# Batch 0's first two tiles as a pair, and later or closer o tiles for batches 2, 3 and 4, in a fused attention and MLP kernel

## The chip, the cores and the metric

One core of one Trainium2 chip. The metric is the device time of one execution in microseconds (us). The kernel before takes 290.79 us (three runs, 290.41 to 290.98).

Engines: PE is TensorE, PEld its weight loads, ACT is ScalarE, DVE is VectorE, POOL is GpSimd, SP is SyncE (here it only issues DMAs).

## The reference

```python
# q, k, v: (8 batches, 8 heads, 576, 64)
kv  = einsum('bhsd,bhse->bhde', k, v)
o   = einsum('bhsd,bhde->bhse', q, kv)
x   = o / sqrt(mean(o*o, -1) + 1e-6) * g_norm        # then (8, 576, 512)
xn  = (x - mean(x)) / sqrt(var(x) + 1e-6) * g_ln
out = x + relu(xn @ w_ch1) @ w_ch2                    # 512 -> 2048 -> 512
```

## The kernel before

Each batch's 576 rows are four tiles of 128; the last 64 rows of two batches make a leftover tile. For each tile, PE computes o from the turned q (`qt`) and the batch's kv. DVE and ACT make x and the centred xc from it. xc is turned to `xT`, for early batches by PE, from batch 2 on by a DMA. `mm1` (line 413) multiplies xT by w1, `mm2` (line 429) the relu by w2. POOL issues the loads of later batches; before each set it copies one element of every tile that has to be ready first (`gate`, line 98), so the copy shows when that tile landed.

An agenda decides when a batch's side work is put among the matmuls of another. `tick()` is called once per slot, about 0.87 us of matmuls:

```python
def at(slot, fn):
    agenda.setdefault(int(slot), []).append((slot, fn))   # the fraction only orders inside a slot

def plan_tile(s, make, turn_at, on_pe):
    ...
    at(s, first)          # o on PE, square on ACT, sum on DVE
    at(s + 2, second)     # root on ACT; reciprocal, y, x, xc on DVE
    at(s + 6, third)      # variance square on ACT
    at(turn_at, fourth)   # xc -> xT

def turn_q_dma(b):
    q_p = kv_in.tile([128, JJ, H, D], bf16, tag="qp", bufs=2)
    nc.vector.tensor_copy(q_p.rearrange("p j h d -> p h j d"), q_in[b % NB])     # line 203
    q_t = qt_pool.tile([128, JJ, HP, 128], bf16, tag="qt", name="qt")
    nc.sync.dma_start_transpose(...)                                             # line 205
```

```python
def mm1(b, t0, n, c0=0, c1=nDe):          # n tiles together, column blocks c0 to c1 of w1
    ...
    per = 4 // n
    for de0 in range(c0, c1, per):
        tick()
        p1 = ps1.tile([128, per, n * 128], f32, tag="p1", name="p1")   # three buffers
        for i in range(per):
            for kk in range(nK):
                nc.tensor.matmul(p1[:, i, :], lhsT=w1_sb[...], rhs=blk[2][:, kk, sl], ...)
        nc.scalar.activation(m1[:, de0:de0 + per, sl], p1, func=AF.Relu)
```

## Time and profile before

| | before |
|---|---|
| time, median of 3 | 290.79 us |
| span of the profiled run | 288.8 us |
| PE busy | 280.9 us, 97% |
| DVE, ACT busy | 149.8 us, 153.2 us |
| waits of PE over 0.2 us after 19 us | four, 1.3 us together |

PE bounds the kernel. The other engines have half their time free, but each tile's chain runs through ACT, DVE and a DMA, and must be ready when PE comes to it. The prediction shows the lines.

A wait of PE is here the excess of the distance between two matmul starts over the usual distance for that shape, unless it is said to be by the profile's count; the profile counts from a matmul's recorded end, which is later, and so gives less.

### The profile page before, as it was taken

What the parts mean: (1) busy time and instruction counts of PE and PEld (TensorE: products, weight loads), DVE (VectorE), ACT (ScalarE), POOL (GpSimd) and SP (SyncE); (2) the same over time, 40 slices, a digit from 0 to 9 for tenths busy, and PEclk for the clock granted to TensorE, in tenths of its full rate; (3) what the DMA queues carried; (4) which work ended last, traced back from release to release, by engine and by line L of the source; (5) the groups of instructions that cost most, each with busy time, mean ns of one, the idle gap of its engine ahead of it and who ended that gap; (6) DMA issues with size and microseconds to landing.
All of it is one profiled execution on the core that took longest, in us unless ns stands there. A gap on an engine that the chain in (4) does not pass through costs nothing.

```text
span 288.8 us, 5753 instructions
## 1 busy us (share of the span) xinstructions
PE 280.9 (97%) x2295; PEld 157.9 (55%) x2295; DVE 149.8 (52%) x331; ACT 153.2 (53%) x333; POOL 41.0 (14%) x69
## 2 busy tenths in 40 slices
PE   7889999999999999999999999999999999999994
PEld 3579756995479644444444444444444444444444
DVE  5774119938897783764376935762578200220022
ACT  3477844985379733872288318921893066016400
POOL 8522510041005004100500032000000000000000
PEclk9999999999999999999999999999999999999999
DMA  7999999979788959996994189947203410230033
GB/s 214 199 206 205 198 190 195 214 112 193 138 173 101 194 108 157 202 159 120 157 217 68 39 152 219 155 84 149 56 18 64 101 36 0 48 81 19 0 73 75
DMA packets 67546, 36.76 MB, mean 127 GB/s; under 512 B 35516, under 2 KB 62524, under 8 KB 67520
## 3 DMA queue, kind: packets, MB, share of 16 engines
q0 software_dynamic: 28528, 17.76, 43.8%
q1 hardware_dynamic: 38480, 17.91, 31.2%
q10 hardware_dynamic: 512, 0.72, 0.7%
q8 instruction: 18, 0.29, 0.4%
q14 instruction: 8, 0.07, 0.1%
HBM read 36.71 MB, written 9.44 MB: 160 GB/s over the span
## 4 chain that ended last, share of the span: by engine, by line
PE 85%; DMA 5%; DVE 5%; ACT 2%; issue 1%; SPq 1%; DVEq 0%; POOLq 0%
PE p L413 41%; PE p L429 37%; PE o_ps L271 2%; DMA v_in<-in_v_dram 2%; DMA qt<-q_p 2%; PE kv_ps L246 2%; DMA xT_blk<-xc 1%; DVE ss L298 1%; ACT m L416 1%; DVE x_blk L322 1%; DVE y L303 1%; DVE o_sb L434 1%; PE p L198 1%; SPq L205 1%; ACT rms L308 0%
## 5 line engine op out<-in xcount | busy, mean ns | idle before, releaser
L413 PE MATMUL p<-xT_blk,w_sb 128*128 128x128 bf16 (+2 forms) x1024 | 131.6, 286 | 0.6 <-DMA xT_blk<-xc 0.2
L429 PE MATMUL p<-w_sb,m 128*128 128x512 bf16 (+2 forms) x608 | 129.1, 368 | 0.0
L416 ACT ACTIVATE m<-p 128x512 bf16<-128x512 f32 x144 | 85.2, 596 | 43.0 <-PE p L413 40.5
L413 PEld LDWEIGHTS <-w_sb 128*128 128x128 bf16 x1024 | 78.7, 98 | 44.9 <-issue 1.5
L429 PEld LDWEIGHTS <-m 128*128 128x128 bf16 x608 | 57.0, 98 | 62.0
L434 DVE SCALAR_TENSOR_TENSOR o_sb<-p,rstd,x_blk 128x512 f32<-128x512 f32 (+2 forms) x38 | 27.3, 720 | 52.2 <-PE p L429 41.2
L277 ACT ACTIVATE sq<-o_ps 128x512 f32<-128x512 f32 x35 | 20.9, 596 | 41.7 <-PE o_ps L271 41.7
L298 DVE TENSOR_REDUCE ss<-sq 128x8 f32<-128x512 f32 x35 | 23.7, 678 | 13.0 <-ACT sq L277 12.9
L340 ACT ACTIVATE dev<-x_blk,st_blk 128x512 f32<-128x512 f32 x36 | 25.7, 714 | 6.2 <-DVE st_blk L326 6.1
L332 DVE SCALAR_TENSOR_TENSOR xc<-x_blk,st_blk,g_ln_sb 128x512 bf16<-128x512 f32 x34 | 25.6, 752 | 1.2
L303 DVE TENSOR_TENSOR y<-o_ps,inv 128x512 f32<-128x512 f32 x33 | 22.8, 692 | 3.4 <-PE p L413 0.5
L322 DVE SCALAR_TENSOR_TENSOR x_blk<-y,g_norm_sb 128x512 f32<-128x512 f32 x33 | 22.8, 692 | 1.1
L315 DVE RECIPROCAL inv<-rms 128x8 f32<-128x8 f32 x36 | 7.2, 201 | 23.0 <-ACT rms L308 23.0
L422 DVE RECIPROCAL rstd<-rstd 128x4 f32<-128x4 f32 x9 | 1.6, 175 | 31.2 <-ACT rstd L421 31.1
L308 ACT ACTIVATE rms<-ss,eps_sb 128x8 f32<-128x8 f32 x36 | 10.7, 296 | 11.5 <-DVE ss L298 11.4
L98 POOL COPY gate<-qt 1x1 bf16<-1x1 bf16 x5 | 0.9, 177 | 106.4 <-DMA qt<-q_p 106.4
L271 PEld LDWEIGHTS <-qt 128*128 128x128 bf16 (+1 forms) x156 | 10.2, 100 | 8.1 <-issue 1.7
L271 PE MATMUL o_ps<-kv_pack,qt 128*128 128x128 bf16 (+1 forms) x156 | 13.7, 220 | 0.2
L198 PE MATMUL p<-fill_sb 128*128 128x512 bf16 x27 | 8.0, 448 | 1.2 <-DVE eps_sb L137 1.2
L340 ACT ACTIVATION_READ_ACCUMULATOR dev<-x_blk,st_blk 128x1 f32 x36 | 6.8, 189 | 0.0
L249 ACT CAST kv_pack<-kv_ps 64x256 bf16<-64x256 f32 x7 | 2.6, 366 | 7.7 <-PE kv_ps L246 7.7
L246 PEld LDWEIGHTS <-k_in 128*64 128x64 bf16 x280 | 5.0, 112 | 2.6 <-issue 2.5
(80 smaller groups left out, 110.5 us busy)
## 6 DMA issues: line engine op xcount, KB each, us to landing
out_dram<-o_sb SPq DMA_DIRECT2D x70, 128.0 KB, 2.4
w_sb<-in_moe_w_ch_dram POOLq DMA_DIRECT2D x8, 512.0 KB, 15.2
q_in<-in_q_dram POOLq DMA_DIRECT2D x7, 320.0 KB, 12.3
k_in<-in_k_dram POOLq DMA_DIRECT2D x7, 320.0 KB, 6.0
v_in<-in_v_dram POOLq DMA_DIRECT2D x7, 320.0 KB, 8.6
q_in<-in_q_dram POOLq DMA_DIRECT2D x8, 256.0 KB, 12.3
k_in<-in_k_dram POOLq DMA_DIRECT2D x7, 256.0 KB, 6.7
v_in<-in_v_dram POOLq DMA_DIRECT2D x7, 256.0 KB, 10.6
```

The lines of the kernel that those rows point to most:

```text
L198: nc.tensor.matmul(p1, lhsT=fill_sb[:, :128], rhs=fill_sb, start=True, stop=True)
L271: nc.tensor.matmul(flat[rows, hp * 128:(hp + 1) * 128], lhsT=lhsT_of(hp), rhs=kvp[:, hp, :], start=True, stop=True)
L277: nc.scalar.activation(self.sq_t, self.o_ps, func=AF.Square)
L298: nc.vector.tensor_reduce(self.ss, self.sq_t, axis=AX.X, op=ALU.add)
L303: nc.vector.tensor_mul(self.y_t, self.o_ps, self.inv().to_broadcast([128, H, D]))
L322: nc.vector.scalar_tensor_tensor(x_blk[:, ts].rearrange("p (h d) -> p h d", h=H), in0=self.y_t, scalar=1.0, in1=g_norm_sb.to_broadcast([12 ...
L332: nc.vector.scalar_tensor_tensor(self.xc_t, in0=x_blk[:, self.ts], scalar=st[:, 1, self.ts:self.ts + 1], in1=g_ln_sb, op0=ALU.add, op1=ALU ...
L340: nc.scalar.activation(dev, x_blk[:, ts], func=AF.Square, bias=st[:, 1, ts:ts + 1], accum_out=st[:, 2, ts:ts + 1])
L413: nc.tensor.matmul(p1[:, i, :], lhsT=w1_sb[:, kk, de * 128:(de + 1) * 128], rhs=blk[2][:, kk, sl], start=(kk == 0), stop=(kk == nK - 1))
L416: nc.scalar.activation(m1[:, de0:de0 + per, sl], p1, func=AF.Relu)
L429: nc.tensor.matmul(p2[:, c0:c1], lhsT=m1s[b][:, de, ts * 128:(ts + 1) * 128], rhs=w2_sb[:, de, c0:c1], start=(de == 0), stop=(de == nDe - 1))
L434: nc.vector.scalar_tensor_tensor(o_sb[:, c0:c1], in0=p2[:, c0:c1], scalar=rstds[b][:, ts:ts + 1], in1=blks[b][0][:, ts, c0:c1], op0=ALU.mu ...
```

## The change

Its intent, as I read it from the diff: fewer and wider matmuls in batch 0, and tiles of batches 2 to 4 placed so that the turned q is there when PE wants it, and batch 3's tiles are done before batch 4's q has to be copied.

```diff
-    for j, s, tn in ((0, 45, 51), (1, 49, 55), (2, 53, 61), (3, 57.5, 64)):
+    for j, s, tn in ((0, 45.7, 51.5), (1, 49.5, 55), (2, 53, 61), (3, 57.5, 64)):
         plan_tile(s, lambda j=j: main_tile(2, j), tn, False)
...
-            o = s + d + (11 if b == 3 else 13) + 5 * j
+            o = s + d + (11.7 + 4.4 * j if b == 3 else (14 if b == 4 else 13) + 5 * j)
...
-    for ts, c0, c1 in ((0, 0, 4), (1, 0, 4), (0, 4, 8), (1, 4, 8), (0, 8, 12), (1, 8, 12),
-                       (2, 0, 12), (0, 12, 16), (1, 12, 16), (2, 12, 16), (3, 0, 16)):
-        mm1(0, ts, 1, c0, c1)
+    for ts, n, c0, c1 in ((0, 1, 0, 4), (1, 1, 0, 4), (0, 2, 4, 12), (2, 1, 0, 12),
+                          (0, 2, 12, 16), (2, 1, 12, 16), (3, 1, 0, 16)):
+        mm1(0, ts, n, c0, c1)
```

## The prediction

> **What bounds the kernel now.** I read the views in this order: the page's totals and slices, the groups of instructions kept apart by shape, the chain of work that ended last in order of time, then the timeline of single engines in the stretches where that chain leaves TensorE.
>
> ```profile
> PE 280.9 (97%) x2295; PEld 157.9 (55%) x2295; DVE 149.8 (52%) x331; ACT 153.2 (53%) x333; POOL 41.0 (14%) x69
> PE   7889999999999999999999999999999999999994
> PEclk9999999999999999999999999999999999999999
> ...
> L413 PE MATMUL p<-xT_blk,w_sb 128*128 128x128 bf16 x512 | 31.2, 219 | 0.4
> L413 PE MATMUL p<-xT_blk,w_sb 128*128 128x256 bf16 x128 | 14.6, 273 | 0.0
> ...
> 19.53 2.69 PE p L413 x48
> 29.41 3.73 PE p L413 x64
> 83.50 4.37 PE p L413 x40
> ```
>
> TensorE (PE) is busy for 97% of the span at full granted clock; from the fourth slice on no slice is below 9 tenths before the last. The mean times 219 and 273 ns are not what a matmul costs: the matmuls overlap. The cost is the distance from one start to the next, and the chain gives it: 48 matmuls of 128 columns take 2.69 us, 56.0 ns each; 40 of 256 columns take 4.37 us, 109.2 ns each. (The 64 in 3.73 us contain one wait of 0.2 us; 3.57 us is the clean figure for 64 elsewhere in the same chain, 55.8 ns.) So only two things can shorten this kernel: less matmul time, or fewer gaps on PE. After the start-up (18 us) I compared every distance between matmul starts with that of its shape. The real waits are four: about 0.24 us at 25.1, 0.21 at 29.15, 0.21 at 82.8, and 0.66 in two pieces at 111.1 to 112.25. They sum to 1.3 us, 0.45% of the time. That is the ceiling for a change that only moves work.
>
> The largest of them:
>
> ```profile
> 106.53 3.10 SPq L205 DMA_TRANSPOSE qt<-q_p  x1
> 109.69 1.26 SPq L352 DMA_TRANSPOSE xT_blk<-xc  x1
> ...
> 111.63 0.40 PE L271 MATMUL o_ps<-kv_pack,qt 128*128 128x128 bf16 x4
> 112.25 1.02 PE L413 MATMUL p<-xT_blk,w_sb 128*128 128x512 bf16 x4 [0.23 <-DMA xT_blk<-xc]
> ...
> 109.69 2.52 DMA xT_blk<-xc
> ```
>
> PE ends batch 2's second product at 111.36, waits for the turned q of batch 4 (qt), does the first o tile of batch 4 (0.22 us) and waits again, for the turned last tile of batch 3 (xT), which lands at 112.21. The SP queue issues qt first and is held 3.1 us by it; so xT is late because qt is, and qt is late because its source, the copy q_p on VectorE (DVE), is:
>
> ```profile
> 98.41 1.50 DVE L298 TENSOR_REDUCE ss<-sq 128x8 f32<-128x512 f32 x2
> 99.83 0.19 DVE L315 RECIPROCAL inv<-rms 128x8 f32<-128x8 f32 x1
> ...
> 103.10 0.19 DVE L315 RECIPROCAL inv<-rms 128x8 f32<-128x8 f32 x1
> ...
> 105.65 0.82 DVE L203 COPY q_p<-q_in 128x2560 bf16<-128x2560 bf16 x1
> ```
>
> From 95.78 to 105.65 DVE has no gap: tiles 2 and 3 of batch 3 and the leftover tile, one after the other.
>
> **What the Trainium skill says.** "TensorE: Matmul & The Clock Gate", section "Wait — 56ns, not 53.3ns?": warm matmuls start N ÷ 2.4 GHz plus about 2.5 ns apart. For 128 columns that is 55.8 ns and for 256 it is 109.2; the trace agrees (55.8 to 56.0, 109.2). So a pair saves one fixed cost of 2.5 ns and nothing more. The same page, "Architectural detail", says that ScalarE (ACT) and DVE take their instructions in strict order; so the order in the program decides, and the trace shows it: ACT's root for tile 2 of batch 3 starts at 95.46, though its sum was ready at 94.32, because a relu and another root stood ahead. "Perfetto Trace Analysis", section "DMA Instruction — HWDGE (DVE, Sync)", says that the recorded time of such an issue doesn't contain the data's movement. The trace agrees: xT's issue took 1.26 us, its landing 2.52.
>
> **The change part by part.**
>
> Part one, the pair. Batch 0's tiles 0 and 1 do 12 of their 16 column blocks of w1 together: 12 x 4 = 48 matmuls of 256 columns in place of 96 of 128. The slots stay 16 and every slot uses the same chunk of w1 as before. Chunks 1, 2 and 3 land at about 17.2, 19.7 and 22.2 us (semaphore arrivals in the trace); their first use is at 19.4, 21.2 and about 26.3. No new wait. The gain is 2 x 55.9 - 109.25 = 2.55 ns per pair, 0.12 us in all. But the slot that starts at 22.5 is followed by the wait at 25.1: ACT did a copy, a square and a root there that waits for DVE's sum, and PE lacks a free product buffer until the next relu. That chain starts with the slot, so its 8 pairs (0.02 us) only lengthen the wait. 40 pairs count: -0.10 us. The waits at 25.1 and 29.15 stay, as what they wait for is untouched. The relus have the same 512 columns.
>
> Part two, batch 2. The agenda runs a function in the whole slot of its number; the fraction only orders functions inside the slot. 45 to 45.7 and 49 to 49.5 therefore move no o tile. Comparing the instruction order of the two kernels engine by engine confirms it: PE's order differs only by the pairs and from batch 3 on; on ACT the roots of tiles 1 and 2 come ahead of the squares for the variance. Those roots start at 68.82 and 73.15, within 0.04 us of the sums that they wait for; the squares had ended at 68.26 and 71.99. So nothing was blocked: 0.00 us. The wait at 82.8 (qt of batch 3, landing at 83.06) stays too, as its o tile stays in slot 66 (66.7).
>
> Part three, batches 3 and 4. Tiles 2 and 3 of batch 3 go from slots 76 and 81 to 75 and 79; the slot is 0.87 us. Tile 2's sum can't come sooner: DVE ends tile 1 at 93.72. But its root now stands behind one relu less and ahead of rstd: right after the variance square, at about 94.79 in place of 95.46. Then on DVE, with the distances measured before: reciprocal at 95.11; 2.63 us to the end of the tile, 97.74; rstd 0.18; tile 3's sum 0.68, ready at 98.62; now a bubble of 0.36 for its root, which used to run beneath the leftover tile's sum; reciprocal at 98.98; 2.61 us, 101.59; the leftover's sum 0.68; the output product 0.66; its reciprocal at 102.93, before 103.10. So q_p, qt and xT come only 0.17 us sooner: xT at 112.04. Meanwhile the first o tile of batch 4 moves from slot 96 to 97. Its 0.22 us lay inside the wait and was free; now it comes after, and costs. -0.17 + 0.22 = +0.05 us. Later stages show no wait: q of batch 5 is turned before 138.5 and used at 141.4.
>
> Sum: -0.10 + 0.00 + 0.05 = -0.05 us. 290.79 - 0.05 = 290.7.
>
> **The rivals.** First, the intent: the tiles closer together free q_p enough that the wait before batch 3's first product ends, and the o tile's later slot keeps qt off the path. For it: 0.66 us is waited there and xT would need to come only 0.7 us sooner than now. Against: DVE has no gap to give back, only the order changes. It would make 290.79 - 0.10 - 0.66 + 0.22 = 290.25. Second, ACT becomes the bound: at 4.4 slots a tile it has 4.4 relus of 0.54, a square 0.55, a variance square 0.8 and a root 0.3, about 4.0 us in 4.1. PE has three product buffers of slack and ACT is idle again from slot 80 on; if it fails, the wait moves into 90 to 96 and costs up to 0.5: 291.2. Third, the extra bubble on DVE is longer than 0.36, q_p is later than before, and the wait grows: 291.0.
>
> **Range and chances.** Three runs before lie within 290.41 to 290.98, so run to run is +-0.3. The rivals lie at -0.5 and +0.4. Range 290.1 to 291.2 for 8 in 10. Two per cent is 5.8 us, over four times all the waits after the start-up, and nothing added costs more than a few tenths: faster 0.01, same 0.98, slower 0.01.
>
> **What would show it.** The shape table: 416 matmuls of 128 columns and 176 of 256. The waits near 25.1 and 29.1 still there, everything from 29.5 on some 0.1 us sooner. o of batch 3's first tile still starts as qt lands. q_p of batch 4 0.2 to 0.3 us sooner than 105.65, and one wait near 111.3 to 112 before the first 512-column product, with xT as its releaser. If that wait is gone, or q_p is 0.5 us sooner or later than I say, step three is wrong; if PE gaps appear at 90 to 96, the second rival holds.

## The result, and the profile after

The changed kernel takes 292.53 us (four runs, 292.24 to 293.57) against 290.60 (four runs). The ratio is 1.0072, 95% interval 1.0044 to 1.010. Ratios here are the mean time of one kernel's fast runs over that of the other's fast runs of the same rounds, so not quite the ratio of the medians. It is slower by 1.9 us: within 2%, but clearly outside the predicted range, which ended at 291.2.

The page of the changed kernel, totals and the PE row of its slices, then its first products by shape (count, busy us, mean ns):

```profile
PE 279.2 (96%) x2222; PEld 157.2 (54%) x2247; DVE 149.6 (51%) x331; ACT 152.6 (52%) x333; POOL 41.4 (14%) x69
...
PE   8689999999989997999999999999999999999994
...
L413 PE MATMUL p<-xT_blk,w_sb 128*128 128x128 bf16 x416 | 25.7, 219 | 0.4
L413 PE MATMUL p<-xT_blk,w_sb 128*128 128x256 bf16 x176 | 20.5, 273 | 0.0
```

The counts 416 and 176 are as planned. Two slices in the row of nines have fallen: an 8 at 80 to 88 us and a 7 at 109 to 117. (Some single matmuls are missing from this trace: PE has 25 fewer than PEld. A distance of exactly two matmuls is such a hole, not a wait.)

The first of these places in the timeline of the kernel before:

```profile
78.09 3.21 SPq L205 DMA_TRANSPOSE qt<-q_p  x1
83.11 0.40 PE L271 MATMUL o_ps<-kv_pack,qt 128*128 128x128 bf16 x4
```

Both places in the changed kernel's timeline, and from the chain of waits the turned last tile of batch 3:

```profile
79.07 3.94 SPq L205 DMA_TRANSPOSE qt<-q_p  x1
84.83 0.40 PE L271 MATMUL o_ps<-kv_pack,qt 128*128 128x128 bf16 x4 [0.79 <-ACT m L416]
84.91 0.18 POOL L98 COPY gate<-qt 1x1 bf16<-1x1 bf16 x1 [17.58 <-DMA qt<-q_p]
...
111.02 1.26 SPq L352 DMA_TRANSPOSE xT_blk<-xc  x1
114.94 1.04 PE L413 MATMUL p<-xT_blk,w_sb 128*128 128x512 bf16 x3 [1.69 <-DMA xT_blk<-xc]
...
111.02 3.87 DMA xT_blk<-xc
```

PE waits 0.95 us for the first o tile of batch 3 in place of 0.21, and 1.85 us between batch 2's second product and batch 3's first; before, that gap was 0.89 us and held an o tile of 0.22. The profile names an ACT relu as the first wait's releaser. But POOL's gate, which waits for the turned q alone, passes at the same moment, 0.08 us later; q landed 5.7 us after its issue. This is the case of several conditions of which the last named is not the guilty one.

The compute chains are not late. Counted from the first o tile of batch 3, the copy q_p of batch 4 comes 22.17 us later (107.00 - 84.83), before 22.54 (105.65 - 83.11). It is the transfers that took longer: the turned q of batch 4 6.6 us in place of 5.1, the turned tile 3.87 in place of 2.52. The view of line 205 (six turned q; the profile gives the landing of five of them before and of four after) shows, before and then after:

```profile
DMA to landing us min/median/max: 4.9/5.0/5.1
```

```profile
DMA to landing us min/median/max: 5.0/5.5/6.6
```

The account from first product to last matmul: before 14.95 to 284.86, 269.91 us; after 16.13 to 287.79, 271.66 us. That is +1.75. Of it -0.09 is the pair stage (18.03 to 17.94 us), +0.74 the first wait, +0.96 the second gap (1.85 - 0.89), +0.22 the o tile that now comes after it: +1.83. The 1.2 us by which this one profile starts later is not in the other three runs, whose spans are 290.5 to 290.8 us.

What slowed the transfers? The page lists a DMA queue of kind "instruction": 18 transfers of 16 KB before (q8), 17 after. These bring PE its program, as the paddings below bear out. The Trainium skill, "Runtime: NRT & Kernel Launch", section "Instruction fetch mechanics", says that programs are refilled in blocks of 16 KiB, 256 instructions, over a DMA queue of the engine's own. The trace agrees in the main: PE's recorded matmuls and weight loads are 4590 before, and 4494 after with each load's matmul counted, 17.9 and 17.6 blocks; the sequencer's own instructions are not in these counts. Taking out 96 instructions moves every later refill. The records of that queue start before at 74.4, 89.2 and 102.8 us, all clear of the turned q of batches 3 (78.1 to 83.1) and 4 (106.5 to 111.6). After, they start at 78.9 and 112.4, beside both. (A second queue of this kind, q14, moves pieces of 8 KB; in none of the traces does one fall inside a turned q.)

The DMA view, 3 us each, begins as batch 3's q is turned: the kernel before from 78.0, the changed one from 78.8. Rows are 40 slices of the mean busy share of 16 engines, and of GB/s.

```profile
DMA  9896959559998969533799999999999999999999
GB/s 218 218 300 137 300 109 246 137 137 246 273 218 164 218 137 273 109 58 51 133 236 208 256 191 246 188 232 171 242 201 212 198 225 208 229 212 225 215 218 215
```

```profile
DMA  0966996969299979992400100000001599999999
GB/s 0 218 164 164 218 218 137 246 137 246 82 246 219 273 164 218 191 246 55 110 0 0 27 0 0 27 27 27 27 27 14 106 195 229 222 222 201 225 212 208
...
q8 instruction: 1, 0.02, 2.5%
```

Before, the dip in the middle is three slices long. After, eleven slices (0.8 us) hold almost nothing: at most a tenth of the engines move, and then all resume together. In the second place (111 to 115 us of the changed kernel) the rate is 8 to 10 GB/s for most of 1.2 us, where the whole set gives over 200: about what one engine in sixteen gives.

```profile
GB/s 220 210 218 220 200 225 218 205 220 205 185 111 54 148 376 212 195 207 177 72 8 0 0 0 8 10 8 10 10 10 8 21 0 0 123 123 82 225 123 246
...
q8 instruction: 1, 0.02, 1.5%
```

This reads as one DMA engine that had the 16 KB refill to do (1.0 to 1.2 us for each of these two) and finishes its share of the turning late, while the other fifteen are done and the transfer counts as landed only with the last. The packet times in the trace fit: the refill of the second place ends at 113.40 us, and from then to 114.17 the turning's packets of 256 bytes end one after the other, some 0.03 us apart. The Trainium skill, "DMA: Bandwidth & Descriptors", section "Issuing engines are not separate DMA queues", says that transfers from different issuers run on the same 16 engines and interleave. Up to here all this is reading. The experiments follow.

### The profile page after: what moved, and what is told of

It reads as the page before. It is cut to its first block, busy times and chain, and to the rows that moved or that the text cites. A ratio compares the mean times of both kernels' runs of the same rounds, so it can differ in the third digit from the quotient of the medians.

```text
span 291.8 us, 5633 instructions
## 1 busy us (share of the span) xinstructions
PE 279.2 (96%) x2222; PEld 157.2 (54%) x2247; DVE 149.6 (51%) x331; ACT 152.6 (52%) x333; POOL 41.4 (14%) x69
## 4 chain that ended last, share of the span: by engine, by line
PE 67%; DMA 17%; issue 10%; DVE 2%; POOL 1%; ACT 1%; SPq 0%; DVEq 0%; POOLq 0%
PE p L413 33%; PE p L429 32%; DMA v_in<-in_v_dram 8%; DMA w_sb<-in_moe_w_ch_dram 5%; DMA q_in<-in_q_dram 3%; PE o_ps L271 2%; DMA xT_blk<-xc 1%; PE kv_ps L246 1%; DVE o_sb L434 1%; DVE ss L298 0%; SPq L205 0%; ACT m L416 0%; DVE q_p L203 0%; DVE x_blk L322 0%; DVE y L303 0%
## 5 line engine op out<-in xcount | busy, mean ns | idle before, releaser
L429 PE MATMUL p<-w_sb,m 128*128 128x512 bf16 (+2 forms) x592 | 126.7, 368 | 1.4 <-issue 0.8
L413 PEld LDWEIGHTS <-w_sb 128*128 128x128 bf16 x976 | 77.7, 98 | 47.2 <-DMA xT_blk<-xc 2.2
L298 DVE TENSOR_REDUCE ss<-sq 128x8 f32<-128x512 f32 x35 | 23.7, 678 | 15.4 <-ACT sq L277 15.4
L246 PE MATMUL kv_ps<-v_in,k_in 128*64 128x64 bf16 x280 | 5.8, 197 | 0.0
```

The lines of the kernel that those rows point to most:

```text
L246: nc.tensor.matmul(kv_ps[hh * D:hh * D + D, hp, :], lhsT=k_in[b % NB][:, h, j, :], rhs=v_in[b % NB][:, h, j, :], start=(j == 0), stop=(j = ...
L298: nc.vector.tensor_reduce(self.ss, self.sq_t, axis=AX.X, op=ALU.add)
L413: nc.tensor.matmul(p1[:, i, :], lhsT=w1_sb[:, kk, de * 128:(de + 1) * 128], rhs=blk[2][:, kk, sl], start=(kk == 0), stop=(kk == nK - 1))
L429: nc.tensor.matmul(p2[:, c0:c1], lhsT=m1s[b][:, de, ts * 128:(ts + 1) * 128], rhs=w2_sb[:, de, c0:c1], start=(de == 0), stop=(de == nDe - 1))
```

## The experiments

Theory R: the loss comes from the refills, moved by the 96 removed PE instructions onto transfers that PE waits for. Rival S: the moved slots cost it. Each run below was timed beside the kernel before on the same chip, and gave correct results.

**The pair alone.** All slots as before, batch 0 as after.

```diff
-        mm1(0, ts, 1, c0, c1)       # before's list of single tiles
+        mm1(0, ts, n, c0, c1)       # the changed kernel's list
```

> Part one alone: batch 0's pair, all agenda slots as before. PE has 96 instructions fewer than before, as the changed kernel has. Theory R (PE's instruction refills, 16 KB each, one per 256 PE instructions, come at other moments and slow the turning transfers they meet): nearly all of the loss is here, 291.6 to 292.4 us, with a refill near 78 to 79 and another near 110 to 113, the wait before batch 3's first o tile 0.7 to 1.0 us in place of 0.21, and the wait before batch 3's first product over 1 us. Rival S (the moved slots cost it: tiles closer together, the o tile no longer hidden): 290.5 us, no longer wait anywhere.

Measured: 291.93 us (six runs) against 290.60, ratio 1.0049 (1.0034 to 1.0064). Refills at 78.6, 97.6 and 114.9; batch 3's q lands 5.9 us after issue and PE waits 1.16 us for it. Batch 4's q lands in 5.0 and the wait at 111 to 114 is short; that part of the expectation missed, and so did the refill expected near 110 to 113. Instead PE waits elsewhere (the profile's timeline of PE):

```profile
102.28 0.82 PE L246 MATMUL kv_ps<-v_in,k_in 128*64 128x64 bf16 x40 [0.38 <-DMA v_in<-in_v_dram]
...
173.49 0.40 PE L271 MATMUL o_ps<-kv_pack,qt 128*128 128x128 bf16 x4 [0.45 <-DMA qt<-q_p]
```

The first is the load of v for batch 4. Its second part was issued 1.1 us later than in the kernel before (this profile's first product is 0.8 us late, and POOL's gates on batch 3's turned q and batch 2's turned tile passed later), and it took 9.5 us in place of 8.1, with the refill of 97.6 inside it. The second is batch 6's q, issued at 166.8, with a refill at 171.4, landing in 6.6 us. The part that saves matmul time loses 1.3 us, most of the changed kernel's 1.9; the two intervals overlap, so the rest is not told apart.

**The slots alone.** Batch 0 as before, agenda as after.

```diff
-        mm1(0, ts, n, c0, c1)       # the changed kernel's list
+        mm1(0, ts, 1, c0, c1)       # before's list
```

> Parts two and three alone: the moved slots, batch 0 without the pair. PE has as many instructions as before. Theory R: 290.4 to 290.9 us, refills at the same moments as before within 0.5 us, turned q of batches 3 and 4 landing 5.0 us after issue. Rival S: 292 to 292.6 us, with the refills where they were and the waits of the changed kernel.

Measured: 290.39 us (five runs), ratio 0.9994 (0.9982 to 1.0007). All turned q with a recorded landing (five of six) land in 4.9 to 5.1 us. Rival S falls.

**The changed kernel with 96 PE instructions put back.** They are tiny matmuls on zeros while PE idles for its first loads.

```diff
-    fill(18)
+    fill(14)
+    small(52)     # 52 matmuls of 64 columns into an unused PSUM tile: 104 PE instructions, less the 8 of 4 fills
```

> The changed kernel with 96 PE instructions put back as tiny matmuls of 64 columns on zeros while PE idles for the first loads (4 of the 18 warming matmuls give way), so that refills meet the same work as before. Theory R: 290.3 to 290.8 us, refills near 74.4, 89 and 102.8, the two long waits gone back to 0.2 and under 0.7 us. Rival S: 292.5 us as the changed kernel.

Measured: 290.54 us, ratio 0.9999 (0.9987 to 1.001). Refills at 74.4, 89.1 and 103.0; the turned q land in 4.9 to 5.1 us; the waits are 0.21 us, and 0.56 us for the turned tile (0.39 by the profile's count). The view of the turned q:

```profile
DMA to landing us min/median/max: 4.9/5.0/5.1
```

Adding 52 useless matmuls, with 4 filling ones taken out, takes the whole loss away.

**The kernel before with 160 PE instructions more.** The same padding, 160 PE instructions, which is 96 fewer counted in blocks of 256.

```diff
-    fill(18)
+    fill(10)
+    small(88)
```

> The kernel before with 160 PE instructions more, again tiny matmuls in the idle start, so that its refills stand where the changed kernel has them (160 more is 96 fewer, counted in blocks of 256). Theory R: 291.5 to 292.5 us, with refills near 78 and 111 and turned q late by 0.7 us and more. Rival S: 290.6 us; if it is slower without longer transfers, the padding itself costs.

Measured: 292.56 us, ratio 1.0064 (1.0051 to 1.0076). The kernel before becomes as slow as the changed one. The view of its turned q, and PE's wait for batch 3's:

```profile
DMA to landing us min/median/max: 5.0/5.3/6.7
...
84.07 0.40 PE L277 MATMUL o_ps<-kv_pack,qt 128*128 128x128 bf16 x4 [0.41 <-DMA qt<-q_p]
```

Its refills come at 79.3, 96.8 and 113.9, the second place later than expected; the losses are at batch 3's q (landing in 5.3 us, a wait of 0.57 us) and again at batch 6's, which lands in 6.7 us; batch 4's, expected late, landed in 5.0. 0.6 us of the loss lies before the first product (15.51 against 14.95 us), where the padding itself may be at work; from there to the last matmul it loses 1.28 us.

**The changed kernel with 48 put back.**

```diff
-    fill(18)
+    fill(16)
+    small(26)
```

> The changed kernel with 48 PE instructions put back, half of what the pair removed. Theory R: the refill that met batch 3's turned q moves some 4 to 5 us sooner, to about 74 us, ahead of that transfer, so the first of the two long waits is 0.2 us again; the refill at about 112 moves to about 106 to 107, where it still touches the start of batch 4's turned q, which lands 0.5 to 1 us late. One of two losses stays: 290.8 to 291.7 us. Rival N (any number of padding instructions helps, by what they do at the start and not by where the refills fall): 290.5 us, as with 96. Rival S: 292.5 us.

Measured: 291.29 us, ratio 1.0016 (1.000 to 1.0031): between the two, as theory R had it (its interval begins at 1.000, so the loss is barely told from none), but not for the reason given. The refills came at 76.2 and 103.5, where I expected about 74 and 107. Both turned q land in 5.0 us. Another refill, at 38.4 us, now falls among the loads of w2, and PE waits for one of them:

```profile
41.97 1.24 PE L435 MATMUL p<-w_sb,m 128*128 128x512 bf16 x5 [0.29 <-DMA w_sb<-in_moe_w_ch_dram]
```

That "some padding helps by itself" is refuted by the 160 above; and which transfer is hit is not to be had by counting to 256 alone.

**A schedule out of the refills' reach.** The changed kernel; batch 3's first o tile really two slots later, batch 3's last tile turned ahead of batch 4's q, batch 4's first o tile in slot 99.

```diff
-            o = s + d + (11.7 + 4.4 * j if b == 3 else (14 if b == 4 else 13) + 5 * j)
-            plan_tile(o, ..., o + 6, False)
+            o = s + d + (13 + 5 * j if b > 4 else ((13, 16.5, 20.5, 24.9) if b == 3 else
+                                                   (16, 20, 24.5, 29))[j])
+            plan_tile(o, ..., 84.5 if (b, j) == (3, 3) else o + 6, False)
```

> The changed kernel, no padding, refills left where they are, with the waits taken out of their reach: batch 3's first o tile really two slots later (slot 68), the turned last tile of batch 3 issued ahead of the turned q of batch 4, and batch 4's first o tile in slot 99. Theory R: the turning transfers that meet refills still land late (5.7 and 6.6 us in place of 5.0), but nobody waits for them; both long waits are gone and 289.5 to 290.0 us come out, ahead of both kernels. Rival P (the refills hold PE itself up, not the transfers): still over 291.5 us.

> The same schedule with 96 PE instructions put back at the start, so that the refills fall as in the kernel before. Theory R: where nobody waits for the transfers, the place of the refills no longer matters: the same as without padding within 0.3 us, 289.5 to 290.0 us. Rival P: 1.5 us or more faster than without padding.

The second has `small(52)` at the start as well. Measured: 292.02 us without padding (ratio 1.0036) and 290.90 with it (0.9997), beside 290.84. Both missed. The two long waits are gone in both profiles, but a new one stands at batch 4's k-v product. Without padding and with it:

```profile
102.19 0.82 PE L246 MATMUL kv_ps<-v_in,k_in 128*64 128x64 bf16 x40 [1.51 <-DMA v_in<-in_v_dram]
```

```profile
101.90 0.82 PE L252 MATMUL kv_ps<-v_in,k_in 128*64 128x64 bf16 x40 [1.20 <-DMA v_in<-in_v_dram]
```

Unpadded, the time is also what rival P said (refills hold PE itself up), but the wait is for v, and the next experiment answers P. The load of v had no slack: its issue waits for batch 2's turned tile. In the changed kernel it landed at 101.8 us and PE, held up before, came to it at 101.9; here PE comes at 100.5 in both runs, and v lands at 102.1 and 101.8. A wait removed upstream had hidden it. That is not all: the second part of v took 9.6 and 9.7 us, in place of 8.1 in the kernel before, and with padding no refill lies inside it. What slowed it there is open.

**The same, with batch 4's k-v product three slots later.**

```diff
-        at(s + d + (1 if b < 5 else 0), lambda b=b: kv_of(b))
+        at(s + d + (4 if b == 4 else 1 if b < 5 else 0), lambda b=b: kv_of(b))
```

> As the schedule before without padding (batch 3's first o tile in slot 68, batch 3's last tile turned ahead of batch 4's q, batch 4's first o tile in slot 99), and batch 4's k-v product three slots later (slot 87): in the last run PE waited 1.4 to 1.7 us there for the load of v, whose issue hangs on batch 2's turned tile and so on the late turned q. Theory R with this cure: no long wait after 30 us, 289.6 to 290.2 us, ahead of both kernels. If something else has to be waited for, the wait moves once more and the time stays above 290.6.

> The same with 96 PE instructions put back at the start. Theory R: within 0.3 us of the run without padding, as no wait is in a refill's reach: 289.6 to 290.2 us. If refills cost in another way than through transfers that are waited for, this is 1 us and more faster than without padding.

Measured: 290.89 us without padding (ratio 1.0006, 0.9989 to 1.0024) and 290.02 with it (0.9971, 0.9958 to 0.9984), beside 290.74. With padding no wait over 0.11 us is left after 30 us, and this version beats the kernel before by 0.7 us (0.29%), and the changed one by more. Without padding batch 3's q still lands in 5.6 us and nobody waits, as meant; but a refill at 42.4 lies among the loads of w2, and PE waits 0.3 us near 41, near 45 (there for w2) and near 60 (for DVE's xc). After 61 us, with eleven refills, PE has no wait over 0.11 us: the refills do not hold PE itself up, and rival P falls. I had said the padding would no longer matter; it still matters by 0.9 us, as the three early waits show: the schedule was put out of reach of later refills only.

**The changed kernel once more.**

> The changed kernel once more. Its profile was of the slowest of four runs, and started its first product 1.2 us later than the kernel before. If that was chance, this profile starts within 0.5 us of before and the time is 292.2 to 292.7 us, with the two long waits and the two late turned q as they were. If it starts 1.2 us late again, the start is part of the loss.

Measured: 292.98 us (four runs, 292.08 to 293.83), ratio 1.0076. This profile starts its first product at 14.82 us, so the late start was chance. The losses fell partly on other transfers, in the timeline of PE:

```profile
84.61 0.40 PE L271 MATMUL o_ps<-kv_pack,qt 128*128 128x128 bf16 x4 [1.08 <-DMA qt<-q_p]
...
102.97 0.82 PE L246 MATMUL kv_ps<-v_in,k_in 128*64 128x64 bf16 x40 [1.17 <-DMA v_in<-in_v_dram]
...
45.59 1.24 PE L429 MATMUL p<-w_sb,m 128*128 128x512 bf16 x5 [0.31 <-DMA w_sb<-in_moe_w_ch_dram]
```

Here the first wait names the turned q itself (it landed in 6.0 us). The second is the v load again, whose second part took 10.3 us in place of 8.1, with a refill at 98.0 inside. The wait before batch 3's first product, 1.85 us in the first profile, is gone, as PE comes there later. Same kernel, same total, other places.

## Why the prediction was wrong

- The bound and the matmul distances held; the ceiling of 1.3 us for gains was not passed (the best run gained 0.7). It said nothing of what could be lost. Two readings were off, without effect on the sum: the list of waits after 18 us leaves one of 0.2 us at 18.4 out, and w1's chunks landed at 17.9, 20.4 and 23.7 us by the profile, not 17.2, 19.7 and 22.2, still before their use.
- Part one: the sum's term of -0.10 us was right: the stage from the first product to batch 0's second took 17.94 us in place of 18.03. But "No new wait" was wrong. The step counted w1's arrivals, the only transfers that the pair itself reads, and not what 96 fewer instructions do to PE's program loads. The pair alone costs 1.3 us.
- Part two, no effect: nothing speaks against it. With the slots alone the wait for batch 3's q stayed (0.21 us), as said.
- Part three: +0.05 us was predicted for the slots; slots alone, from first product to last matmul, gave 269.89 against 269.91 us: -0.02. q_p came 0.38 us sooner and not 0.17, so xT did too; the o tile then cost its 0.22. Differences as small as -0.02 and +0.05 are inside the +-0.3 from run to run, so the times alone don't confirm the sum.
- The failed step is therefore the one under the whole sum: the landing times of the turned q (4.97 us) and of the turned tile (2.52 us) were carried over from the profile before as constants. They became 5.7, 6.6 and 3.87 us. With refills put back in place by padding, the changed kernel took 290.54 us, where 290.7 was predicted: nothing else as large as this step was missed.
- The rivals: the first (tiles closer, wait gone) and the second (ACT as the bound) did not happen. The third, q_p later, didn't either: the wait grew with q_p sooner. None of the three named the transfers.
- The test named in the prediction, "q_p 0.2 to 0.3 us sooner", has to be read from batch 3's first o tile; in absolute time it was 1.35 us later, because of the late start and the first wait.

What is shown: the number of PE instructions ahead decides where the refills fall, and with it whether the turned q that PE waits for land late (the two paddings, one each way; the padding also changes the first 15 us a little). All twelve profiles agree with it: 35 turned q had no refill between issue and landing, and each landed in at most 5.15 us; 20 had one, and 15 of these took 5.3 to 6.7 us. The other five took 4.9 to 5.0, so a refill beside a transfer does not always delay it. That one DMA engine does the refill while fifteen wait is read from the DMA view and the packet times, and was not tested by itself. Open is what sets a refill's exact moment, and with it which transfer is hit: in the kernel before PE starts 247 instructions from one refill to the next on average, but 166 to 283 in single cases, and two profiles of the changed kernel differ in the places.

## What to carry to other kernels

When a change removes or adds PE instructions in a kernel with no slack on its transfers, look at the DMA queue of kind "instruction" before and after: every later program refill moves, and a turned q that met one here mostly landed 0.3 to 1.7 us later. Take a transfer's landing time as a range, and look for slack where PE waits. Slack is not easily had: here it took two schedules to get back to the time of the kernel before, 290.89 us, and the gain of 0.7 us came only with padding as well. Test with padding in an idle stretch: if a few dozen useless matmuls bring the time back, the schedule was not at fault.

## What the Trainium skill lacked or had wrong

- "Runtime: NRT & Kernel Launch", section "Instruction fetch mechanics", calls the cost of crossing a 16 KiB boundary mostly hidden. For PE itself it was (eleven refills and no wait over 0.11 us after 61 us in the last schedule without padding); but the refill delays other transfers. Of 20 turned q with a refill inside, 15 landed in 5.3 to 6.7 us, against at most 5.15 without, and the pair alone, 96 PE instructions fewer, cost 1.3 us of 290.6.
- The same section gives blocks of 256 instructions, which the count of refills bears out (18 for 4590, 17 for 4494), but not how far the moment of a single refill strays: they came 166 to 283 instructions apart in the kernel before, and 48 instructions of padding moved one from 78.9 to 76.2 us and another from 112.4 to 103.5.
- "DMA: Bandwidth & Descriptors" says that issuers share the 16 engines, but not what a 16 KB program refill (about 1 us, in the DMA view at a rate of one engine) does to a DMA transpose that uses all of them: in the changed kernel it held one up for 0.7 and one for 1.5 us.
